# Two attention layers in one kernel: K chunks in halves, wider weighted-V products, a 28-column normalization, and four more score banks on VectorE

## The chip, the cores and the metric

The kernel runs on one core of a Trainium2 chip. The core has five engines that run at their own pace and wait for each other through semaphores: TensorE (PE: matmuls, with a separate row PEld for loading weights), ScalarE (ACT: exponentials), VectorE (DVE: elementwise work, copies and reductions), GpSimd (POOL) and SyncE (SP, which here only issues DMAs). Matmul results go to PSUM, eight banks of 512 fp32 columns by 128 partitions. The metric is the device time of one execution in microseconds, the median of several runs.

## The reference, cut to what matters

Two independent attention layers on 2048 positions of width 448, with 16 heads of 28; their outputs stand side by side.

```
# A: full attention, 16 query heads, one shared K and V
q = (x @ wq) per head;  k = x @ wk;  v = x @ wv          # k, v: 2048 x 28
p = softmax(q @ k.T * 28**-0.5)                          # 16 x 2048 x 2048
outA = (p @ v, heads side by side) @ wo
# B: local attention, window of 8 positions, 2 apart
q, k, v = x @ wqkv per head
logits[s, w] = q[s] . k[s - 2*w] * 28**-0.5   (masked before the start)
outB = (sum_w softmax(logits)[s, w] * v[s - 2*w], heads side by side) @ wo
```

A's softmax has 16 x 2048 x 2048 = 67 million exponentials, and they make up most of the work.

## The kernel before, in words

**A's main loop.** Scores are computed transposed: 128 keys on the partitions, 512 queries on the columns, one PSUM bank. One such bank is a *unit*; there are 1024, ordered by query chunk `sc` (4), group of four heads `t` (4), key block `tb` (16) and head in the group `j` (4). A pair (sc, t) of 64 units is called a head group here; there are 16, numbered 4·sc + t. Units go through a ring of two *slots* (`SLOTS`, line 26): slot 0 is banks 0, 1, 2, slot 1 is banks 3, 4. TensorE fills a slot (`qk`, L847, or L844 in a form that uses the whole array), ScalarE takes the exponential of the slot in one instruction (L864) into one of seven `expT` buffers, and TensorE multiplies the result by V (L910), accumulating in bank 5 (`PVBANK`). A slot can be filled again only once it is read. 1024 units in steps of 3 and 2 make 410 exponentials.

**Banks taken by VectorE.** In some rounds (one round is both slots) the third bank of slot 0 is left out of ScalarE's exponential, which is then 1024 columns wide instead of 1536. VectorE copies that bank out (`d_x`, L943), and for every two such banks runs a polynomial of three instructions over 1024 columns (L953, L955, L957) that gives the same exponentials as bf16 bits. `OFF_AT` (line 41) lists the rounds in each head group: six for the groups in `SIX`, four for the others, 84 banks in all.

**End of a head group** (`a_quad_end`). VectorE transposes bank 5 out (L971), takes the reciprocal of the denominators (L976, column 28 of 32), multiplies (L977), transposes back (L980), and after each fourth group TensorE applies `wo` (L994).

**The head of the kernel** (`a_head`). K is computed in four chunks of 512 positions, the first in two halves of 256 (`KF`). A half has its matmuls (L675), its squares (L682 on ScalarE for chunk 0; a copy L685 and a product L687 on VectorE for the later chunks), a matmul that adds the squares' sum (L689) and an add that writes `kT` (L692). The squares give a factor per key, which `a_v` applies to V: four one-column matmuls (L750) into **the bank of the chunk's last K part**, then an exponential on ScalarE (L754, `gcol`), then `v_aug` (L756 to L762). The bank is free only after L754. In chunk 0 the two query halves and the two K halves take banks out of `HB`, that is 0 to 3.

**B's pipeline.** Sixteen blocks of 128 positions: q and k (L1035, L1040), v (L1050, L1054) through DRAM into a shifted copy `Vsh`; products of q and shifted k (L1076), summed by four-column matmuls (L1085); softmax (L1097 to L1117); products of V and weights for two of the eight window slots at a time (L1130, four per block), summed and transposed on TensorE (L1136), then `wo` (L1143) and the store (L1148). Its work fills what A leaves of VectorE and TensorE.

**What sets the order.** Nothing is ordered at run time: `Sched.run` is a list scheduler in the builder, which simulates five queues with durations written by hand and emits each engine's instructions in the order that it finds. An instruction has a priority `pr` (lower goes first) and an earliest time `rel`. Score groups, their exponentials and the `d_x` copies are the *ring*, whose turn is protected from longer work (`limit`). `area` measures how many matmul columns TensorE ran in the last 2.5 us; where it is low, filler is put in (matmuls on `warm` data: L418, L441, L839) or score groups take the whole-array form. So any changed duration or priority reorders all that follows.

```
SLOTS = ((0, 1, 2), (3, 4))
PVBANK = 5
XBANKS = (6, 7)
SIX = (1, 2, 3, 5, 6, 8, 9, 11, 12, 14)
OFF_AT = {q: (0, 2, 3, 5, 7, 8) if q in SIX else (0, 2, 5, 7) for q in range(1, 16)}
PSTT = -35.0
```

Of the kernel before, what the change touches and what calls it, by code (L numbers as in the profile page):

```python
# [30 lines left out]
TAILB = (4, 0)  # L31
WARM = 8
KF = 256
QT = 27.0


EL, EP, EQ = -10.141819427815111, -5.83493489876537, 4.836063470359898
EOFF = 8
A2 = SCALE * 1.4426950408889634
SIX = (1, 2, 3, 5, 6, 8, 9, 11, 12, 14)  # L40
OFF_AT = {q: (0, 2, 3, 5, 7, 8) if q in SIX else (0, 2, 5, 7) for q in range(1, 16)}
OFF_AT[15] = (0, 2, 3, 5)
OFF_AT[0] = (4, 5, 6, 7)
LATE = 2
PSTT = -35.0
DR = 2
DX = 3

# [50 lines left out]
class Sched:  # L99
# [6 lines left out]
    IDLE = 1400.0  # L106
    FULL = {2: 1400.0, 3: 1300.0}
    LOW = 1200.0
    QKT = 0.32
    EPS = -0.04  # L110
    FILL = None
# [37 lines left out]
    def run(self, engines):  # L149
# [15 lines left out]
        locks = {"dve": 0.0, "gp": 0.0}  # L165

        def area(T):
            return sum(d for (t1, d) in recent if t1 > T - self.WIN) / self.WIN

        def ready(o):  # L170
            t = o.rel
# [210 lines left out]
def t_dve_ps(n):  # L382
    return 0.067 + 1.04e-3 * n
# [22 lines left out]
class Gen:  # L406
# [142 lines left out]
    def consts(self):  # L549
# [40 lines left out]
                                               base=-PAD, pattern=[[0, H], [2, WIN]], channel_multiplier=1), W=["mask0"], pr=-8.05)  # L590
        a("dve", 1.0, lambda e: e.memset(g.wo4[:, :, :], 0.0), W=["wo4"], pr=-3)
        a("gp", 0.2, lambda e: e.memset(g.kTB[:, :, 0:PAD], 0.0), W=["kTBpad"], pr=-8.05)

    def loads(self):
        g, a = self, self.s.add
# [52 lines left out]
              R=[("wq", min(t, 1)), "wqz", ("d_x", 0, 0), ("d_x", 0, 1)], W=[("wq4", t)], pr=-6 if t == 0 else 1.2 + t)  # L648

    HB = (0, 1, 2, 3)  # L650
    TB = (4, 5, 6, 7)
    LB = (6, 7)
    VPR = 0.5
# [3 lines left out]
    def a_head(self):  # L657
        g, a = self, self.s.add
        g.kz_ops = {}
        for n, pr, rel in ((WARM, -30, 0.0), (1, -15, 4.6)):  # L660
            def warm(e, n=n):
                for _ in range(n):
                    r = e.matmul(g.bank(3), g.warm[:, 0:128], g.warm[:, :], start=True, stop=True)  # L663
                return r
            u = Use(f"warm{n}", (3,))
            a("pe", 0.43 * n, warm, R=["warm"], use=u, pr=pr, rel=rel)
        for c in range(NCH):
            pr = -9 if c == 0 else c
            HB = g.HB if c == 0 else g.LB
            if c < 2:  # L670
                g.a_tr(c)
            for k, (lo, n) in enumerate(((0, KF), (KF, 512 - KF)) if c == 0 else ((0, 512),)):
                u = Use(f"K{c}.{k}", HB, late=c == 0)
                for kt in range(4):
                    a("pe", t_mm(n), lambda e, u=u, c=c, kt=kt, lo=lo, n=n: e.matmul(  # L675
                        g.bank(u.bank, n), g.wk4[:, kt, :], g.xT_A[:, kt, 512 * c + lo:512 * c + lo + n],
                        start=kt == 0, stop=kt == 3),
                      R=[("xT", c, kt), "wk4"], W=[u], use=u, pr=pr + 0.1 * k, rel=8.0 * min(c, 1), dense=n)
                ksq = g.k_sq[:, c % 2, lo:lo + n]
                kc = g.kT[:, 512 * c + lo:512 * c + lo + n]  # L680
                if c == 0:
                    a("act", t_act(n), lambda e, u=u, ksq=ksq, n=n: e.activation(ksq, g.bank(u.bank, n), ACT.Square),  # L682
                      R=[u, "d_u"], W=[("k_sq", c % 2, k)], use=u, pr=-100)
                else:
                    a("dve", t_dve_ps(n), lambda e, u=u, kc=kc, n=n: e.tensor_copy(out=kc, in_=g.bank(u.bank, n)),  # L685
                      R=[u], W=[("kT", c, k)], use=u, pr=min(pr, -2))
                    a("dve", t_dve_2x(n), lambda e, ksq=ksq, kc=kc: e.tensor_tensor(out=ksq, in0=kc, in1=kc, op=ALU.mult),  # L687
                      R=[("kT", c, k), "d_u"], W=[("k_sq", c % 2, k)], pr=-2)
                a("pe", t_mm(n), lambda e, u=u, ksq=ksq, n=n: e.matmul(  # L689
                    g.bank(u.bank, n), g.hq[:, 2, :], ksq, start=False, stop=True, skip_group_check=True),  # L690
                  R=[("k_sq", c % 2, k), "hq", "d_u"], W=[u], use=u, pr=pr + 0.1 * k, dense=n)
                a("dve", t_dve_ps(n) + 0.08, lambda e, u=u, kc=kc, n=n: e.tensor_scalar(  # L692
                    out=kc, in0=g.bank(u.bank, n), scalar1=g.cols[:, 0:1], scalar2=None, op0=ALU.add),
                  R=["kadd"], W=[("kT", c, k)], use=u, pr=min(pr, -2) - (1 - k if c == 0 else 0))
            kc = g.kT[:, 512 * c:512 * c + 512]
            g.kz_ops[c] = [a("dve", Lock(0.3), lambda e, j=j, c=c, kc=kc: e.tensor_scalar(
                out=g.kz[:, j, 512 * c:512 * c + 512], in0=kc, scalar1=g.cols[:, 8 + j:9 + j], scalar2=None, op0=ALU.mult),
                R=["jmask"] + g.keys_of(c), W=[("kz", c)], pr=4 + c) for j in range(4)]
            if c == 0:
                g.a_q(0, first=True)  # L700
            g.a_v(c, u)

    def key_of(self, tb):

        return ("kT", tb // 4, int(KF <= 128 * tb < 512))

    def keys_of(self, c):
        return sorted({self.key_of(4 * c), self.key_of(4 * c + 3)})
# [1 line left out]
    def a_tr(self, c):  # L710

        g, a = self, self.s.add
        for kts in ((0,), (1,), (2,), (3,)) if c == 0 else ((0, 1), (2, 3)):
            u = Use(f"T{c}{kts[0]}", g.TB[kts[0]:kts[0] + 1] if c == 0 else g.LB)
            for i, kt in enumerate(kts):
                for b in range(4):
                    a("pe", 0.1, lambda e, u=u, i=i, kt=kt, b=b: e.transpose(  # L717
                        g.psb[:, 1024 * u.bank + 512 * i + 128 * b:1024 * u.bank + 512 * i + 128 * b + 128],
                        g.xst[:, 4 * c + b, XB0[kt]:XB0[kt] + 128], g.ident[:, :]),
                      R=[("xst", c), "ident"], use=u, pr=-16 if c == 0 else -2, dense=128)  # L720
            for i, kt in enumerate(kts):
                dst = g.xT_A[:, kt, 512 * c:512 * c + 512]
                src = lambda u=u, i=i: g.psb[:, 1024 * u.bank + 512 * i:1024 * u.bank + 512 * i + 512]
                if c or kt % 2:
                    a("dve", 0.335, lambda e, src=src, dst=dst: e.tensor_copy(out=dst, in_=src()),
                      W=[("xT", c, kt)], use=u, pr=-2 if c else -9)
                else:
                    a("act", t_act(512), lambda e, src=src, dst=dst: e.activation(dst, src(), ACT.Copy),
                      W=[("xT", c, kt)], use=u, pr=-110)

    def a_v(self, c, uk):

# [201 lines left out]
    def d_exp(self, bank, slot, sib):  # L934
# [11 lines left out]
        o.ring = True  # L946
        o.sib = sib
        if h:
            pp = 10.0 + 26.7 * (4 * g.quad[0] + g.quad[1]) + PSTT
            u, v = g.d_u[:, :], g.d_v[:, :]  # L950
            lo = xx.bitcast(mybir.dt.uint16).rearrange("p (c two) -> p c two", two=2)[:, :, 0]
            di = [("d_x", m % DX, 0), ("d_x", m % DX, 1)]
# [9 lines left out]
    def a_quad_end(self, sc, t, hf=None):  # L962
# [11 lines left out]
        g.evacs = [o]  # L974
        pt = g.PV_T[:, t % 2, :].rearrange("p (b e) -> p b e", e=32)
        a("dve", 0.16, lambda e: e.reciprocal(out=g.rden[:, t % 2, bs], in_=pt[:, bs, DH]), R=kk("PV"), W=kk("rden"), pr=p0)  # L976
        a("dve", t_dve_1x(w), lambda e: e.tensor_tensor(  # L977
            out=g.oN[:, bs, :], in0=pt[:, bs, :], in1=g.rden[:, t % 2, bs].unsqueeze(2).to_broadcast([128, b, 32]), op=ALU.mult),
          R=kk("PV") + kk("rden"), W=[("oN", x) for x in keys], pr=p0)
        a("dve", 0.09 + 1.04e-3 * w, lambda e: e.transpose(  # L980
            out=g.oTn[:, t, cs], in_=g.oN[:, :, :].rearrange("p b e -> p (b e)")[:, cs]),
          R=[("oN", x) for x in keys], W=[("oTn", t, x) for x in keys], pr=p0)
# [80 lines left out]
    def b_logits(self, k):  # L1063
# [1 line left out]
        T = g.B0 + g.BSTEP * k  # L1065
        c, b = k // 4, k % 4
        pr = T + 12
        for t in range(4):
            R = [("qTB", c % 2, t), ("kTB", t, c)]
            if k == 0:  # L1070
                R += ["kTBpad"]
            elif b == 0:
                R += [("kTB", t, c - 1)]
            qv = g.qTB[:, c % 2, t, 128 * b:128 * b + 128].unsqueeze(1).to_broadcast([KC, WIN, 128])
            kv = g.ap(g.kTB[:, t, :], 128 * k, [[2, WIN], [1, 128]])
            op = a("dve", t_dve_2x(1024), lambda e, t=t, qv=qv, kv=kv: e.tensor_tensor(  # L1076
                out=g.prodT[0:KC, t, :, :], in0=qv, in1=kv, op=ALU.mult), R=R, W=[("prodT", t)], pr=pr, rel=T)
            if k == 0:
                op.deps.update(o for i in range(2) for o in g.s.rd.get(("xst", i), ()) if o.eng == "pe")
        u = Use(f"L{k}", XBANKS, spare=128)  # L1080
# [41 lines left out]
    def b_out(self, k):  # L1122
# [1 line left out]
        T = g.B0 + g.BSTEP * k  # L1124
        par, b = (k // 2) % 2, k % 2
        pr = T + 30
        for qr in range(4):
            Vv = g.Vsh[:, k % 2, 2 * qr:2 * qr + 2, :].rearrange("p w (d h) -> p w d h", h=H)
            av = g.a_n[:, par, b, 2 * qr:2 * qr + 2, :].unsqueeze(2).to_broadcast([128, 2, DH, H])
            a("dve", t_dve_2x(2 * D), lambda e, qr=qr, Vv=Vv, av=av: e.tensor_tensor(  # L1130
                out=g.prod2[:, 2 * qr:2 * qr + 2, :].rearrange("p w (d h) -> p w d h", h=H), in0=Vv, in1=av, op=ALU.mult),
              R=[("Vsh", k % 2), ("a_n", par, b)], W=[("prod2", qr)], pr=pr, rel=T)
        u = Use(f"BT{k}", XBANKS)
        for t in range(4):
            for w in range(WIN):
                a("pe", 0.056, lambda e, u=u, t=t, w=w: e.matmul(  # L1136
                    g.bank(u.bank, 128, 128 * t, p1=KC), g.prod2[:, w, KC * t:KC * t + KC], g.ident[:, :],
                    start=w == 0, stop=w == WIN - 1), R=[("prod2", w // 2), "ident"], W=[u], use=u, pr=pr, dense=128).extra = 0.045
        a("dve", t_dve_ps(512), lambda e, u=u: e.tensor_copy(out=g.oT[:, k % 2, :], in_=g.bank(u.bank, p1=KC)),
          W=[("oT", k % 2)], use=u, pr=-1)  # L1140
        u = Use(f"BP{k}", XBANKS)
# [53 lines left out]
```

## Time and profile before

| | |
|---|---|
| median of 13 runs | 451.98 us (449.22 to 465.8) |
| the profiled execution | 451.61 us, of which 449.9 span |
| mean granted TensorE clock | 0.992 of full speed |
| ScalarE busy | 435.3 us (97%), of it L864 430.3 in 410 instructions |
| VectorE busy | 419.0 us (93%) in 680 instructions |
| TensorE busy | 410.1 us (91%) |
| GpSimd busy | 14.0 us (3%) |
| DMA | 27.30 MB, mean 61 GB/s |
| first exponential starts | 10.07 us |

In the rows of the profile, `L864` is a line of the kernel, `expT<-ps` what is written and read, and an arrow in brackets names the instruction whose end released a waiting engine. "Busy" of an engine is the time in which at least one of its instructions is under way; successive instructions of one engine overlap by a little, so the cost of one in a full queue is the distance between two starts, not its duration.

### The profile page before, as it was taken

To read this page: it belongs to the slowest core of one execution; us is meant where nothing else is said; L and a number is where in the kernel's file an instruction comes from. 1 tells how busy PE (TensorE), PEld (TensorE's weight loads), DVE (VectorE), ACT (ScalarE), POOL (GpSimd) and SP (SyncE) were. 2 spreads that over 40 slices of the span, in tenths; PEclk is the share of its full clock that TensorE was granted. 3 is DMA by queue.
4 is the path that set the end of the run, shared out by engine and by line. 5 is a ranking of instruction groups with operands and counts; after the bars stand their busy time and mean duration, and the time that the engine had idled before them with its cause. 6 is when DMAs were issued, how large, how long until landed. Compare 5 with 4: busy or idle time off the path is not lost.

```text
span 449.9 us, 8992 instructions
## 1 busy us (share of the span) xinstructions
PE 410.1 (91%) x3755; PEld 159.1 (35%) x3800; DVE 419.0 (93%) x680; ACT 435.3 (97%) x431; POOL 14.0 (3%) x36
## 2 busy tenths in 40 slices
PE   8888999999899999999999989989989989898894
PEld 4222232322353423323443443334324433442441
DVE  7889999899999999999979999998999998999963
ACT  4899999999999999999999989999999999999995
POOL 6112000000000000000000000000000000000000
PEclk9999999899999999999999989999999999999999
DMA  7946202000261312002121330023000330220001
GB/s 170 191 63 171 38 12 92 1 2 10 93 128 34 103 41 84 12 10 83 34 71 52 96 100 12 12 74 102 12 21 22 103 103 22 83 92 12 12 12 42
DMA packets 39988, 27.30 MB, mean 61 GB/s; under 512 B 15518, under 2 KB 39592, under 8 KB 39948
## 3 DMA queue, kind: packets, MB, share of 16 engines
q1 hardware_dynamic: 37452, 24.06, 19.4%
q0 software_dynamic: 816, 1.53, 1.6%
q10 hardware_dynamic: 1680, 1.13, 0.8%
q8 instruction: 30, 0.49, 0.5%
q14 instruction: 10, 0.08, 0.1%
HBM read 18.06 MB, written 5.52 MB: 52 GB/s over the span
## 4 chain that ended last, share of the span: by engine, by line
ACT 94%; PE 4%; DVE 1%; issue 0%
ACT expT L864 94%; PE ps L663 1%; PE ps L844 1%; PE ps L847 1%; ACT e_t L1111 0%; PE ps L781 0%; PE ps L994 0%; PE ps L910 0%; PE ps L717 0%; DVE qT L800 0%; PE ps L796 0%; PE ps L675 0%; ACT outA L1001 0%; DVE PV_T L971 0%; DVE oTn L980 0%
## 5 line engine op out<-in xcount | busy, mean ns | idle before, releaser
L864 ACT ACTIVATE expT<-ps 128x1024 bf16<-128x1024 f32 (+1 forms) x410 | 430.3, 1337 | 4.3 <-PE ps L847 3.0
L847 PE MATMUL ps<-qT,kT 32*128 32x512 bf16 (+1 forms) x1043 | 152.0, 372 | 22.1 <-ACT expT L864 16.9
L910 PE MATMUL ps<-expT,v_aug 128*32 128x512 bf16 (+1 forms) x1000 | 95.2, 377 | 0.3 <-DVE mx L1097 0.3
L847 PEld LDWEIGHTS ps<-qT,kT 32*128 32x128 bf16 x1043 | 37.9, 91 | 115.8 <-ACT expT L864 103.4
L943 DVE TENSOR_SCALAR d_x<-ps 128x512 f32<-128x512 f32 x84 | 57.2, 680 | 7.1 <-PE ps L847 6.1
L953 DVE SCALAR_TENSOR_TENSOR d_u<-d_x 128x1024 f32<-128x1024 uint16 x42 | 50.8, 1210 | 0.4 <-PE ps L689 0.3
L957 DVE SCALAR_TENSOR_TENSOR dexp<-d_u,d_x 128x1024 int16<-128x1024 f32 x42 | 50.9, 1211 | 0.0
L955 DVE SCALAR_TENSOR_TENSOR d_u<-d_u,d_x 128x1024 f32<-128x1024 f32 x42 | 50.8, 1209 | 0.1
L1136 PE MATMUL ps<-ident,prod 128*112 128x128 bf16 x512 | 46.2, 227 | 0.1
L910 PEld LDWEIGHTS ps<-expT,v_aug 128*32 128x32 bf16 x1000 | 24.1, 93 | 53.2 <-issue 50.3
L1076 DVE TENSOR_TENSOR stage<-qTB,kTB 112x1024 bf16<-112x1024 bf16 x64 | 41.9, 675 | 0.3 <-PE ps L1085 0.3
L1136 PEld LDWEIGHTS ps<-ident,prod 128*112 128x112 bf16 x512 | 35.0, 130 | 19.0 <-issue 17.1
L1130 DVE TENSOR_TENSOR prod<-Vsh,a_n 128x896 bf16<-128x896 bf16 x64 | 37.3, 611 | 0.9 <-PE ps L1136 0.8
L1035 PE MATMUL ps<-xT_B,wqkv 128*128 128x512 bf16 x115 | 35.8, 384 | 1.2 <-issue 0.8
L1085 PEld LDWEIGHTS ps<-ones,stage 112*128 112x128 bf16 x512 | 18.6, 96 | 10.0 <-issue 5.9
L1085 PE MATMUL ps<-ones,stage 112*128 112x4 bf16 x512 | 21.8, 167 | 0.1
L994 PE MATMUL ps<-wo,oTn 128*128 128x448 bf16 x64 | 17.4, 356 | 1.8 <-DVE oTn L980 1.7
L781 PE MATMUL ps<-xT_A,wq 128*128 128x512 bf16 (+1 forms) x60 | 18.3, 378 | 0.4 <-issue 0.3
L1143 PE MATMUL ps<-wo_B,oT 112*128 112x448 bf16 x64 | 18.5, 358 | 0.1
L1050 PE MATMUL ps<-wqv,xT_B 128*128 128x448 bf16 x64 | 17.8, 357 | 0.5 <-DVE qT L800 0.5
L971 DVE STREAM_TRANSPOSE PV_T<-ps 128x512 f32<-128x512 f32 (+1 forms) x17 | 11.5, 678 | 5.8 <-PE ps L910 5.7
L1035 PEld LDWEIGHTS ps<-xT_B,wqkv 128*128 128x128 bf16 x128 | 9.9, 97 | 18.1 <-issue 12.7
(107 smaller groups left out, 282.8 us busy)
## 6 DMA issues: line engine op xcount, KB each, us to landing
Vsh<-v_scratch SPq DMA_DIRECT2D x16, 896.0 KB, 4.6
v_scratch<-Vst SPq DMA_DIRECT2D x16, 112.0 KB, 1.7
out_dram<-outB SPq DMA_DIRECT2D x16, 112.0 KB, 1.7
out_dram<-outA SPq DMA_DIRECT2D x15, 112.0 KB, 1.7
stage<-in_A_x_dram ACTq DMA_DIRECT2D x2, 448.0 KB, 4.1
wqkv<-in_B_wqkv_dram SPq DMA_DIRECT2D x1, 672.0 KB, 5.1
wo_B<-in_B_wo_dram POOLq DMA_DIRECT2D x4, 98.0 KB, 2.8
wo<-in_A_wo_dram POOLq DMA_DIRECT2D x4, 98.0 KB, 2.6
```

Source lines behind the costliest of these rows:

```text
L847: r = e.matmul(g.bank(b0 + i, nq, nq * k), g.kT[32 * j:32 * j + 32, 128 * tb:128 * tb + 128], g.qT[32 * j:32 * j + 32, sc % 2, t, q0:q0 + ...
L864: x = a("act", t_exp(w), lambda e, b0=b0, w=w, n=n: e.activation(g.expT[:, n % ERING, 0:w], g.ps[:, 512 * b0:512 * b0 + w], ACT.Exp, scale ...
L910: x = e.matmul(g.bank(PVBANK, nq, q0, p0=32 * j, p1=32 * j + 32), g.v_aug[:, w, tb, :], src[:, nq * k:nq * k + nq], start=first, stop=last ...
L943: o = a("dve", t_dve_ps(512), lambda e: e.tensor_scalar(out=xx[:, 512 * h:512 * h + 512], in0=g.bank(bank), scalar1=-128.0 * A2, scalar2=1 ...
L953: a("dve", t_dve_1x(1024), lambda e: e.scalar_tensor_tensor(out=u, in0=lo, scalar=EP * F, in1=lo, op0=ALU.add, op1=ALU.mult), R=di, W=["d_ ...
L955: a("dve", t_dve_1x(1024), lambda e: e.scalar_tensor_tensor(out=v, in0=u, scalar=EQ * F * F, in1=lo, op0=ALU.add, op1=ALU.mult), R=["d_u"] ...
L957: a("dve", t_dve_1x(1024), lambda e: e.scalar_tensor_tensor(out=out, in0=v, scalar=EL / F ** 3, in1=xx, op0=ALU.mult, op1=ALU.subtract), R ...
L1035: a("pe", t_mm(512), lambda e, u=u, t=t, kt=kt, w=w: e.matmul(g.bank(u.bank), g.wqkv[:, kt, w * D + KC * t:w * D + KC * t + 128], g.xT_B[: ...
L1076: op = a("dve", t_dve_2x(1024), lambda e, t=t, qv=qv, kv=kv: e.tensor_tensor(out=g.prodT[0:KC, t, :, :], in0=qv, in1=kv, op=ALU.mult), R=R ...
L1085: r = e.matmul(g.bank(u.bank, 128).rearrange("p (h w) -> p h w", w=WIN)[:, 4 * t:4 * t + 4, w], g.prodT[0:KC, t, w, :], g.ones4[:, :], sta ...
L1130: a("dve", t_dve_2x(2 * D), lambda e, qr=qr, Vv=Vv, av=av: e.tensor_tensor(out=g.prod2[:, 2 * qr:2 * qr + 2, :].rearrange("p w (d h) -> p ...
L1136: a("pe", 0.056, lambda e, u=u, t=t, w=w: e.matmul(g.bank(u.bank, 128, 128 * t, p1=KC), g.prod2[:, w, KC * t:KC * t + KC], g.ident[:, :], ...
```

## The change

- K's second chunk is also computed in halves (`KSPLIT = 2`), and the score groups wait for the half that they need (`key_of`). The two K halves of chunk 0 get fixed banks, 2 and 5 (`KB`), so the four columns of `gcol` are now in bank 5. The keys of the dependency tracking are named by half.
- B's products of V and weights take four window slots at a time (`WS = 4`): two instructions per block in place of four.
- The normalization multiplies the 28 columns of each head in place of all 32; `oN` is zeroed once on GpSimd.
- Head groups 10 and 13 join `SIX`: 88 banks on VectorE in place of 84.
- The polynomial instructions of the first four VectorE banks get a priority later by `D0 = 30`.
- Between 14 and 50 us of the plan, `area` is taken 150 lower (`EARLY`).
- `TS = 1` and `TACT` are names for what was there before.

```diff
+KSPLIT = 2
+TS = 1
+WS = 4
+TACT = ((0, 2), ())
...
-SIX = (1, 2, 3, 5, 6, 8, 9, 11, 12, 14)
+SIX = (1, 10, 13, 2, 3, 5, 6, 8, 9, 11, 12, 14)
...
+D0 = 30.0
...
+    EARLY = 150.0
...
-            return sum(d for (t1, d) in recent if t1 > T - self.WIN) / self.WIN
+            return sum(d for (t1, d) in recent if t1 > T - self.WIN) / self.WIN - (self.EARLY if 14 < T < 50 else 0.0)
...
+        a("gp", 0.2, lambda e: e.memset(g.oN[:, :, :], 0.0), W=["oNz"], pr=-8.04)
...
+    KB = ((2,), (5,))
...
-            for k, (lo, n) in enumerate(((0, KF), (KF, 512 - KF)) if c == 0 else ((0, 512),)):
-                u = Use(f"K{c}.{k}", HB, late=c == 0)
+            for k, (lo, n) in enumerate(((0, KF), (KF, 512 - KF)) if c < KSPLIT else ((0, 512),)):
+                u = Use(f"K{c}.{k}", g.KB[k] if c == 0 else g.LB, late=c == 0)
+                uk, x0 = (u, c, k), 0
...
-        return ("kT", tb // 4, int(KF <= 128 * tb < 512))
+        return ("kT", tb // 4, int(tb // 4 < KSPLIT and KF <= 128 * (tb % 4)))
...
-            pp = 10.0 + 26.7 * (4 * g.quad[0] + g.quad[1]) + PSTT
+            pp = 10.0 + 26.7 * (4 * g.quad[0] + g.quad[1]) + PSTT + (D0 if g.nd <= 4 else 0.0)
...
-        a("dve", t_dve_1x(w), lambda e: e.tensor_tensor(
-            out=g.oN[:, bs, :], in0=pt[:, bs, :], in1=g.rden[:, t % 2, bs].unsqueeze(2).to_broadcast([128, b, 32]), op=ALU.mult),
-          R=kk("PV") + kk("rden"), W=[("oN", x) for x in keys], pr=p0)
+        a("dve", t_dve_1x(b * DH), lambda e: e.tensor_tensor(
+            out=g.oN[:, bs, 0:DH], in0=pt[:, bs, 0:DH], in1=g.rden[:, t % 2, bs].unsqueeze(2).to_broadcast([128, b, DH]), op=ALU.mult),
+          R=kk("PV") + kk("rden") + ["oNz"], W=[("oN", x) for x in keys], pr=p0)
...
-        for qr in range(4):
-            Vv = g.Vsh[:, k % 2, 2 * qr:2 * qr + 2, :].rearrange("p w (d h) -> p w d h", h=H)
-            av = g.a_n[:, par, b, 2 * qr:2 * qr + 2, :].unsqueeze(2).to_broadcast([128, 2, DH, H])
-            a("dve", t_dve_2x(2 * D), lambda e, qr=qr, Vv=Vv, av=av: e.tensor_tensor(
+        for w in range(0, WIN, WS):
+            Vv = g.Vsh[:, k % 2, w:w + WS, :].rearrange("p w (d h) -> p w d h", h=H)
+            av = g.a_n[:, par, b, w:w + WS, :].unsqueeze(2).to_broadcast([128, WS, DH, H])
+            a("dve", t_dve_2x(WS * D), lambda e, w=w, Vv=Vv, av=av: e.tensor_tensor(
...
```

## The prediction, made before the result was known

> **What bounds the kernel now.** I read the chain that ended last first, then ScalarE's timeline, then VectorE's, then busy time by stage.
>
> ```profile
> ACT 94%; PE 4%; DVE 1%; issue 0%
> ```
>
> ScalarE's exponentials (L864) carry 94% of the span, from 10.07 us to about 443 us. So the end moves in three ways only: fewer columns on ScalarE, less waiting between exponentials, or a changed head or tail. The start of the row, from ScalarE's timeline (start, duration, engine, line; idle time before in brackets):
>
> ```profile
> 10.07 1.45 ACT L864 ACTIVATE expT<-ps 128x1536 bf16<-128x1536 f32 x1 [1.19 <-PE ps L847]
> 11.41 0.17 ACT L754 ACTIVATE gcol<-ps 128x4 f32<-128x4 f32 x1
> 12.33 1.45 ACT L864 ACTIVATE expT<-ps 128x1536 bf16<-128x1536 f32 x1 [0.75 <-PE ps L847]
> 13.68 1.02 ACT L864 ACTIVATE expT<-ps 128x1024 bf16<-128x1024 f32 x1
> 14.58 1.46 ACT L864 ACTIVATE expT<-ps 128x1536 bf16<-128x1536 f32 x1
> 15.91 1.04 ACT L864 ACTIVATE expT<-ps 128x1024 bf16<-128x1024 f32 x1
> 17.44 1.02 ACT L864 ACTIVATE expT<-ps 128x1024 bf16<-128x1024 f32 x1 [0.48 <-PE ps L847]
> ```
>
> Start to start, 1024 columns take 0.90 us (13.68 to 14.58) and 1536 take 1.33 us (14.58 to 15.91): one bank of 512 costs 0.43 us. The widths show that the slots do not alternate here: 1536 follows 1536, then 1024 follows 1024, so each time the same banks are used twice running and ScalarE waits for their refill. The price, against these steps: 12.33 − 11.41 − 0.06 for gcol = 0.86 us, and 17.44 − 15.91 − 0.90 = 0.63 us. Why the order broke stands in TensorE's timeline:
>
> ```profile
> 11.57 0.39 PE L839 MATMUL ps<-warm 128*128 128x512 bf16 x1 [0.22 <-ACT gcol L754]
> 11.89 0.61 PE L847 MATMUL ps<-qT,kT 32*128 32x512 bf16 x5
> ```
>
> L839 is the filler that opens a score group, and writes the first bank of its slot. It waited for gcol, whose four columns lie in the bank of K's second half: slot (3, 4) could not be filled before gcol, and the five matmuls at 11.89 are both slots at once.
>
> Apart from this, I summed ScalarE's start-to-start distances less 0.90, 1.33, 0.06 (gcol) and 0.31 (L1111): what remains is 1.46 us from 80 to 90 us, 1.82 us from 260 to 270 us, and about 0.13 us per 10 us elsewhere. The two lumps are the clock; busy time by stage (PE, PEld, DVE, ACT and POOL busy us with their instructions, then the granted clock, DMA share and GB/s):
>
> ```profile
> 78.00:80.00 2.00, 1.80 (x42) 1.14 (x38) 2.00 (x4) 2.00 (x3) 0.00 (x0) 1.00 0.03 8
> 80.00:82.00 2.00, 1.52 (x12) 0.43 (x13) 2.00 (x6) 1.79 (x3) 0.00 (x0) 0.65 0.00 0
> 82.00:84.00 2.00, 2.00 (x10) 0.39 (x6) 1.64 (x3) 1.89 (x3) 0.00 (x0) 0.50 0.00 0
> ```
>
> So a clock dip costs 1.3 to 1.7 us.
>
> **The change, part by part.** The sum is against the profiled execution: 451.61 us, a span of 449.9 and 1.7 around it. The median of 13 runs is 451.98, 0.37 above.
>
> *K's first chunk to banks 2 and 5.* Its second half and gcol leave bank 3, so slot (3, 4) can be filled right after the first score group, at about 10.0. Bank 5's first user is a transpose whose copy ends before K's matmuls at 7.3; its next, the first weighted-value product, comes at 15.07, after gcol at 11.58. Nothing new is queued. Gain 0.86; bounds 0 (another hold on the slot) and 0.9. I take 0.86, since the trace names the waiter.
>
> *K's second chunk in halves.* With alternation restored, the second wait goes as well, if the keys are there. The seventh exponential is the first that needs the second chunk (keys from 512 on). It would start at about 16.8 instead of 18.36, and its score matmuls must start by 16.2. Today the keys are ready at 16.80, after a cast of 0.60, a square of 0.33, a matmul of 0.39 and an add of 0.66: too late by 0.6. Halved, the first half's ops shorten by 0.27, 0.13, 0.12 and 0.27 (the 256-wide add takes 0.39 start to start), together 0.8: ready at about 16.0. VectorE pays three more instructions of 0.07 to 0.13, about 0.3 us, in a stretch with idle time (14 to 16 us is 1.37 busy of 2.00). Gain 0 to 0.63; I take 0.5, as the margin is only 0.2. Without the halves, the first gain would largely be paid back here.
>
> *D0.* The first two polynomial pairs (L953 to L957) get lower priority. At 27.65 such an op of 1.13 stood ahead of the last chunk's add (28.79), whose keys now are wanted some 1.5 us earlier, near 29.0, instead of at 30.5; they came at 29.54. It is cover for the same gain: 0 by itself, up to 0.5 lost without it.
>
> *Four more banks to VectorE* (two heads' groups, 10 and 13, from four to six). ScalarE: four exponentials of 1536 become 1024, 4 × 0.43 = 1.72 us. All of it is on the path. VectorE's price, from its timeline:
>
> ```profile
> 407.45 0.61 DVE L1130 TENSOR_TENSOR prod<-Vsh,a_n 128x896 bf16<-128x896 bf16 x1
> 407.98 0.68 DVE L943 TENSOR_SCALAR d_x<-ps 128x512 f32<-128x512 f32 x1
> 408.58 1.21 DVE L957 SCALAR_TENSOR_TENSOR dexp<-d_u,d_x 128x1024 int16<-128x1024 f32 x1
> 409.72 0.61 DVE L1130 TENSOR_TENSOR prod<-Vsh,a_n 128x896 bf16<-128x896 bf16 x1
> ```
>
> An eviction holds the engine 0.60, a polynomial op 1.13. Four evictions and two pairs of three ops: 2.4 + 6.8 = 9.2 us. Some more weighted-value groups of about 0.4 us go to TensorE, idle 40 us in all.
>
> *Four-slot products.* 64 become 32. [...] A transposing matmul (L1136) now waits for a product of 1.0 instead of 0.53, and score matmuls behind it in TensorE's order with it; such waits are 0.7 us in all today, off the chain: 0, at worst 0.7 more.
>
> *28 columns.*
>
> ```profile
> L977 DVE TENSOR_TENSOR oN<-PV_T,rden 128x512 bf16<-128x512 f32 x15 | 10.3, 684 | 0.2
> L977 DVE TENSOR_TENSOR oN<-PV_T,rden 128x256 bf16<-128x256 f32 x2 | 0.8, 424 | 0.1
> ```
>
> 260 ns for 256 columns, so 64 fewer save 0.065: 15 × 0.065 + 2 × 0.03 = 1.0 us of VectorE, of which 0.03 is in the tail. The zeroing on GpSimd (0.2 to 0.5 by its rows) falls in its idle 3.26 us before 11.65.
>
> *VectorE's account*: +9.2 − 2.2 − 1.0 + 0.3 = +6.3 us, against 30.9 idle. By stage (VectorE busy, instructions, clock, DMA):
>
> ```profile
> 92.00:119.00 27.00, 27.00 (x39) 1.00 0.03 10
> 282.00:309.00 27.00, 26.64 (x44) 1.00 0.14 44
> 361.00:389.00 28.00, 26.79 (x45) 1.00 0.16 51
> 416.00:443.00 27.00, 19.09 (x28) 1.00 0.06 19
> ```
>
> The two stages that take the work have 0.4 and 1.2 us to spare for 4.6 each, so B's work slides back into the last stage, which has 7.9. B's last store is issued at 437.05 and A's last at 447.44; slid by 3 to 6 us, B's still comes first. Full stages seem to cost nothing: from 92 to 119 VectorE has no idle time and ScalarE's remainder is 0.13; groups with six banks average 0.30 (dips apart), those with four 0.30.
>
> *EARLY* lowers the measured activity by 150 between 14 and 50 us of the plan, so TensorE gets more filler there. [...]
>
> Sum: −0.86 − 0.5 − 1.72 − 0.03 + 0.2 = −2.9: 448.7 on the profiled run, 449.1 on the median. I forecast 448.9.
>
> **The rivals.** *(1) The start keeps its waits.* The halves come late or another chunk's keys do: 1.36 is not gained, 448.9 + 1.36 = 450.3. For it: margins of 0.2 us, and VectorE full from 16 us on. Against it: the named waiter. *(2) Slower: VectorE becomes the bound in groups 10 and 13.* Evictions (L943) arrive late, slot (0, 1, 2) is not refilled during the 0.90 us of the other slot, and ScalarE waits. If nothing can slide, the overflow is (4.6 − 0.4) + (4.6 − 1.2) = 7.6 us: 448.9 + 7.6 = 456.5; it decides once more than half of that cannot slide (2.9 cancels the gain, 5.2 makes it clearly slower). For it: 99% busy there. Against it: 92 to 119 us, and B's products there are not due soon. *(3) The dips shift.* The whole order of instructions is new; one dip fewer gives 447.4, none 445.9, one more 450.4.
>
> **How the numbers follow.** About 0.5% (2.3 us; 449.7 and 454.2) is what a measurement of this kernel can tell from no change. Forecast 0.58 (own range 447.4 to 450.2, by the bounds of the K halves and EARLY), rival 1 0.19, rival 2 0.11, fewer dips 0.12. Faster: most of the forecast (0.48), fewer dips 0.12, a little of rival 1 (0.05): 0.65. Same: 0.10 + 0.14 = 0.24. Slower: 0.11. The range leaves out rival 2 and the extreme of fewer dips: 446.6 to 452.0.
>
> **What would show it.** Right: widths alternate 1536, 1024 from the first exponential, with no gap over 0.2 us before 20 us; 117 exponentials of 1536 and 88 evictions; L1130 32 times at about 1.08 us; VectorE near 425 us busy. Wrong: a wait on L692 near the seventh exponential or near 29 us (rival 1); L847 waiting for L943, with gaps at 280 to 390 us (rival 2); more or fewer stages with a clock of 0.5 (rival 3).

## The result, and the profile after

446.77 us (median of 11 runs, 446.65 to 447.14) against 451.97 us (median of 48 runs): a ratio of 0.9893, with a 95% interval of 0.9866 to 0.9919. The profiled execution of the changed kernel took 446.72 us, with a span of 444.9. The forecast was 448.9 with a range of 446.6 to 452.0: the right sign, but 5.2 us gained where 3.1 were forecast.

The row with the shares of the chain that ended last still belongs to ScalarE:

```profile
ACT 93%; PE 3%; DVE 3%; DMA 0%; issue 0%
```

Its first rows, from ScalarE's timeline taken in narrow windows (a row with x2 is the named exponential and the one behind it):

```profile
10.13 1.45 ACT L872 ACTIVATE expT<-ps 128x1536 bf16<-128x1536 f32 x1 [1.18 <-PE ps L855]
11.47 0.17 ACT L762 ACTIVATE gcol<-ps 128x4 f32<-128x4 f32 x1
11.53 1.03 ACT L872 ACTIVATE expT<-ps 128x1024 bf16<-128x1024 f32 x1
12.43 2.39 ACT L872 ACTIVATE expT<-ps 128x1536 bf16<-128x1536 f32 x2
13.76 2.40 ACT L872 ACTIVATE expT<-ps 128x1024 bf16<-128x1024 f32 x2
14.66 2.42 ACT L872 ACTIVATE expT<-ps 128x1536 bf16<-128x1536 f32 x2
15.99 2.43 ACT L872 ACTIVATE expT<-ps 128x1024 bf16<-128x1024 f32 x2
```

The widths now alternate, with starts 0.90 and 1.33 us apart and no wait. TensorE fills both slots at once as soon as the first keys are there, nearly two microseconds before gcol:

```profile
9.69 0.60 PE L855 MATMUL ps<-qT,kT 32*128 32x512 bf16 x5 [0.18 <-DVE kT L700]
```

The same three stages as before (PE, PEld, DVE, ACT and POOL busy, then clock, DMA share, GB/s): the clock is whole, with TensorE *less* busy than before in the stage ahead of the first dip, 1.39 us for 1.80. (In the two stages behind it the kernel before ran at a lower clock, 0.65 and 0.50: there a lone matmul of 512 columns, L796, took 0.61 us, and 0.39 at the full clock.)

```profile
78.00:80.00 2.00, 1.39 (x14) 0.34 (x10) 2.00 (x3) 2.00 (x3) 0.00 (x0) 1.00 0.00 0
80.00:82.00 2.00, 1.50 (x12) 0.50 (x12) 1.87 (x5) 2.00 (x4) 0.00 (x0) 1.00 0.00 0
82.00:84.00 2.00, 1.87 (x12) 0.48 (x11) 2.00 (x3) 2.00 (x3) 0.00 (x0) 1.00 0.00 0
```

VectorE's groups, the product and the normalization (count, busy us, mean ns, idle time before):

```profile
L1139 DVE TENSOR_TENSOR prod<-Vsh,a_n 128x1792 bf16<-128x1792 bf16 x32 | 34.1, 1077 | 0.4 <-PE ps L1145 0.4
L985 DVE TENSOR_TENSOR oN<-PV_T,rden 128x448 bf16<-128x448 f32 x15 | 9.2, 611 | 0.2
```

The product takes 1.08 us, as forecast. From start to start in a full queue it is 1.002 us, where a two-slot one took 0.535: 896 more elements take 0.467, which leaves 0.068 in each product beside its elements. VectorE's busy time in the stages shown before, the later ones shifted by the 5 us that they now come earlier:

```profile
92.00:119.00 27.00, 26.82 (x39) 1.00 0.12 38
277.00:304.00 27.00, 26.71 (x41) 1.00 0.14 44
356.00:384.00 28.00, 27.83 (x42) 1.00 0.16 50
411.00:438.00 27.00, 20.61 (x31) 1.00 0.05 15
```

VectorE is now 97.5 to 99.6% busy from 30 us to 410 us, taken in four stretches. It is busy 423.9 us in all, 4.9 more than before.

**Where the time went**, profile against profile, with the start-to-start account of the prediction (waits are what is left of ScalarE's distances after the steps of 0.90, unrounded 0.903, 1.33, 0.06 and 0.31):

| part | before | after | difference, us |
|---|---|---|---|
| first exponential | 10.07 | 10.13 | +0.06 |
| waits before 20 us | 1.53 | 0.00 | −1.53 |
| four exponentials from 1536 to 1024 columns | 121 wide | 117 wide | −1.71 |
| waits near the two clock dips | 1.37 + 1.79 | none | −3.16 |
| all other waits | 4.59 | 5.59 | +1.00 |
| from the last exponential's start to the end | 6.83 | 7.24 | +0.41 |
| span | 449.85 | 444.93 | −4.9 |

The row of the dips says too much. Of the first 1.37 us, a wait of 0.27 ended at 80.36 us, before the clock fell at 80.59; and the profiled run with its two dips took 451.61 us against 449.22 for the fastest, so the two together cost 2.4 us. Some 0.8 of the +1.00 in the row below it is therefore only a matter of where a wait is booked.

The runs say the same without the trace. The kernel before has a lowest group of runs, 449.22 to 449.29, with a mean clock of 0.996 to 0.999, and others above it in steps, down to a clock of 0.947. The changed kernel has only runs with a clock of 0.996 to 1.000. Lowest against lowest the gain is 449.22 − 446.65 = 2.6 us; the rest of the 5.2 is dips that no longer come. Below, "lowest" is the fastest run of a kernel; in each kernel but after_sparse its listed clock is at least 0.996. The kernel before, measured beside every experiment, had a lowest of 449.22 everywhere but beside no_d0, same_order_single, all_groups and ts2, which ran on another chip, where it was 449.56; so about 0.3 us of the distances given for these four is not theirs.

### The profile page after: what moved, and what is told of

Same layout as the page of the kernel before. It is cut to its first block, busy times and chain, and to the rows that moved or that the text cites. A ratio compares the mean times of both kernels' runs of the same rounds, so it can differ in the third digit from the quotient of the medians.

```text
span 444.9 us, 8974 instructions
## 1 busy us (share of the span) xinstructions
PE 409.1 (92%) x3755; PEld 158.7 (36%) x3794; DVE 423.9 (95%) x661; ACT 433.0 (97%) x431; POOL 14.7 (3%) x37
## 3 DMA queue, kind: packets, MB, share of 16 engines
q0 software_dynamic: 816, 1.53, 1.6%
## 4 chain that ended last, share of the span: by engine, by line
ACT 93%; PE 3%; DVE 3%; DMA 0%; issue 0%
ACT expT L872 92%; PE ps L671 1%; DVE kz L704 1%; ACT e_t L1120 1%; PE ps L855 1%; DVE kT L700 0%; DVE d_x L951 0%; DMA out_dram<-outA 0%; DVE qT L808 0%; PE ps L683 0%; PE ps L725 0%; PE ps L918 0%; DVE kT L693 0%; PE ps L789 0%; DVE d_u L695 0%
## 5 line engine op out<-in xcount | busy, mean ns | idle before, releaser
L872 ACT ACTIVATE expT<-ps 128x1024 bf16<-128x1024 f32 (+1 forms) x410 | 428.2, 1354 | 1.3 <-PE ps L855 1.2
L855 PE MATMUL ps<-qT,kT 32*128 32x512 bf16 (+1 forms) x1047 | 153.2, 372 | 21.1 <-ACT expT L872 17.1
L918 PE MATMUL ps<-expT,v_aug 128*32 128x512 bf16 (+1 forms) x996 | 95.5, 376 | 0.2
L855 PEld LDWEIGHTS ps<-qT,kT 32*128 32x128 bf16 x1047 | 38.4, 91 | 118.2 <-ACT expT L872 102.4
L951 DVE TENSOR_SCALAR d_x<-ps 128x512 f32<-128x512 f32 x88 | 59.8, 679 | 0.8 <-PE ps L855 0.3
L965 DVE SCALAR_TENSOR_TENSOR dexp<-d_u,d_x 128x1024 int16<-128x1024 f32 x44 | 53.4, 1213 | 0.1
L963 DVE SCALAR_TENSOR_TENSOR d_u<-d_u,d_x 128x1024 f32<-128x1024 f32 x44 | 53.3, 1212 | 0.1
L961 DVE SCALAR_TENSOR_TENSOR d_u<-d_x 128x1024 f32<-128x1024 uint16 x44 | 53.3, 1212 | 0.0
L1145 PE MATMUL ps<-ident,prod 128*112 128x128 bf16 x512 | 48.2, 227 | 0.7 <-DVE lg L1108 0.6
L918 PEld LDWEIGHTS ps<-expT,v_aug 128*32 128x32 bf16 x996 | 24.6, 93 | 53.1 <-issue 50.5
L1043 PE MATMUL ps<-xT_B,wqkv 128*128 128x512 bf16 x118 | 37.2, 384 | 0.7 <-issue 0.6
L1139 DVE TENSOR_TENSOR prod<-Vsh,a_n 128x1792 bf16<-128x1792 bf16 x32 | 34.1, 1077 | 0.4 <-PE ps L1145 0.4
L1094 PEld LDWEIGHTS ps<-ones,stage 112*128 112x128 bf16 x512 | 16.7, 96 | 7.5 <-issue 5.4
L1094 PE MATMUL ps<-ones,stage 112*128 112x4 bf16 x512 | 19.3, 167 | 0.0
L979 DVE STREAM_TRANSPOSE PV_T<-ps 128x512 f32<-128x512 f32 (+1 forms) x17 | 11.5, 677 | 4.0 <-PE ps L918 4.0
```

Source lines behind the costliest of these rows:

```text
L855: r = e.matmul(g.bank(b0 + i, nq, nq * k), g.kT[32 * j:32 * j + 32, 128 * tb:128 * tb + 128], g.qT[32 * j:32 * j + 32, sc % 2, t, q0:q0 + ...
L872: x = a("act", t_exp(w), lambda e, b0=b0, w=w, n=n: e.activation(g.expT[:, n % ERING, 0:w], g.ps[:, 512 * b0:512 * b0 + w], ACT.Exp, scale ...
L918: x = e.matmul(g.bank(PVBANK, nq, q0, p0=32 * j, p1=32 * j + 32), g.v_aug[:, w, tb, :], src[:, nq * k:nq * k + nq], start=first, stop=last ...
L951: o = a("dve", t_dve_ps(512), lambda e: e.tensor_scalar(out=xx[:, 512 * h:512 * h + 512], in0=g.bank(bank), scalar1=-128.0 * A2, scalar2=1 ...
L961: a("dve", t_dve_1x(1024), lambda e: e.scalar_tensor_tensor(out=u, in0=lo, scalar=EP * F, in1=lo, op0=ALU.add, op1=ALU.mult), R=di, W=["d_ ...
L963: a("dve", t_dve_1x(1024), lambda e: e.scalar_tensor_tensor(out=v, in0=u, scalar=EQ * F * F, in1=lo, op0=ALU.add, op1=ALU.mult), R=["d_u"] ...
```

## The experiments

The twelve runs ask which of the table's rows belongs to which edit. My theory was the prediction's: three gains on ScalarE's chain (start, columns, dips) with VectorE's extra work hidden; the rivals were that VectorE is the bound, and that another edit or the new order itself made the difference. Undoing an edit makes the builder plan the whole order anew, so each such run shows the edit *and* a new plan. Two runs keep the changed kernel's order fixed and change only what is issued in it.

### The start

**no_k**: after, with `KSPLIT = 1` and chunk 0's halves in `HB`.

```diff
-KSPLIT = 2
+KSPLIT = 1
-                u = Use(f"K{c}.{k}", g.KB[k] if c == 0 else g.LB, late=c == 0)
+                u = Use(f"K{c}.{k}", g.HB if c == 0 else g.LB, late=c == 0)
```

> The changed kernel with its K part undone: the second chunk whole and the first chunk's halves back in banks 0 to 3. My theory: the two waits at the start (0.86 and 0.63 us) come back and the rest of the sum stays, so about 446.8 + 1.0 to 1.5 = 447.8 to 448.3 us, with 1536 after 1536 in ScalarE's first rows. Rival (the gain at the start is paid back later, by the 0.23 and 0.28 us that the changed profile shows at 23 and 31 us): at most +1.0. Rival (the dips of the clock went because of the K part): runs between 448 and 452, with a clock of 0.992.

Measured: 453.74 us (lowest 452.44). The two waits are back to the hundredth: 0.86 and 0.62, 1.54 us before 20 us. But the loss is 5.8 us lowest against lowest. The profile splits it: first exponential 0.3 later, the start 1.5, other waits 1.2 (one of 1.15 at 128 us), the end after the last exponential 2.5 (9.8 us instead of 7.2). The profiled run also has two dips, with waits of 1.34 and 1.69 us, and five of the seven runs have a clock below 0.996. The start is as stated; the rest came with the new plan.

**before_kb**: before, with only the banks changed.

```diff
-            HB = g.HB if c == 0 else g.LB
...
-                u = Use(f"K{c}.{k}", HB, late=c == 0)
+                u = Use(f"K{c}.{k}", ((2,), (5,))[k] if c == 0 else g.LB, late=c == 0)
```

> The kernel before with one edit: the two K halves of chunk 0 in banks 2 and 5. My theory: the exponentials alternate from the first on, and of the first wait of 0.86 and the second of 0.63 us the first goes and part of the second stays, because the second chunk's keys are whole (ready near 16.8, wanted at 16.2): last exponential 0.9 to 1.4 us earlier, dip-free time about 448.0 us against 449.2. Rival: the wait moves in full to the second chunk's keys, and the dip-free time is 449 us or more.

Measured: 450.74 us, lowest 450.39, which is 1.2 us more than the kernel before's lowest. The rival was right: the first wait is gone and a single one of 1.33 us stands in front of the first exponential that needs the second chunk. The add on VectorE:

```profile
17.13 0.75 DVE L691 TENSOR_SCALAR kT<-ps,cols 128x512 bf16<-128x512 f32 x1 [0.45 <-PE ps L688]
```

and TensorE's score matmuls behind it:

```profile
17.94 0.60 PE L846 MATMUL ps<-qT,kT 32*128 32x512 bf16 x5
```

The whole chunk's keys are written at 17.13 to 17.88, and the score matmuls start at 17.94. In the changed kernel the first half's keys are written at 15.06 to 15.54, and the seventh exponential starts at 16.89 without a wait. So banks and halves are worth something only together: 1.53 with both, 0.18 with the banks alone.

**no_d0**: after, with `D0 = 0`.

> The changed kernel without the later priority of the first two polynomial pairs. My theory of the prediction: 0 to 0.5 us at the keys of the last chunk (a wait before the exponential near 30 us), so 446.7 to 447.2 us if the rest of the plan comes out alike. Rival (what a re-planned order does at the end and to the clock outweighs the edit, as in the other re-planned versions): 448 us or more, with the loss after 50 us.

Measured: 453.90 us, lowest 453.25. Its profiled execution fell into long dips later on, so only its first 50 us are read. VectorE:

```profile
29.02 1.22 DVE L961 SCALAR_TENSOR_TENSOR d_u<-d_x 128x1024 f32<-128x1024 uint16 x1
30.15 0.75 DVE L700 TENSOR_SCALAR kT<-ps,cols 128x512 bf16<-128x512 f32 x1
```

ScalarE:

```profile
31.71 1.02 ACT L872 ACTIVATE expT<-ps 128x1024 bf16<-128x1024 f32 x1 [1.30 <-PE ps L855]
```

A polynomial op of 1.1 us stands ahead of the last chunk's add, and the exponential behind those keys waits 1.48 us in all; in the changed kernel the wait at this place is 0.28. D0 covers 1.2 us, where the prediction allowed 0.5. The other 5.4 us came with the new plan.

### VectorE's account

**ten_groups**: after, with `SIX` as before (84 banks).

> The changed kernel with 84 banks on VectorE (head groups 10 and 13 with four). My theory: four exponentials are 0.43 us longer, 446.8 + 1.7 = 448.5 us, nothing else. Rival (VectorE is close to being the bound, and its fuller queue costs waits on the score groups): less than +1.2, since those waits go with the four banks. Rival (dips come back with this order): spread over 2 us with a clock below 0.996.

Measured: 449.10 us, lowest 448.75: 2.1 to 2.3 us more. This plan has the changed kernel's waits up to 200 us to within 0.02 us at the large ones (0.22 at 23 us, 0.39 at 194), so this is the cleanest of the undone edits. The last exponential starts 2.0 us later: 1.71 for the columns and 0.36 for waits, less 0.07 at the first exponential. So moving four more banks costs ScalarE nothing in these two plans.

**narrow_dve**: after, with `WS = 2` and 32 columns, planned anew.

> The changed kernel with two-slot products and 32-column normalization: VectorE has 2.2 + 1.0 = 3.2 us more to do, ScalarE nothing. My theory: these savings only pay for the four banks and lie beside ScalarE, so 446.8 to 447.3 us, and VectorE's busy time rises from 423.9 to about 427. Rival (VectorE is the second bound): +1 to +3 us, with L855 waiting for L951 more than the 3.2 us of the changed profile.

Measured: 449.68 us, lowest 449.58, 2.9 us more. By the number alone the rival wins, but the rows of the end (one timeline of all engines; VectorE's last, then SyncE's DMA issue) show how:

```profile
446.39 0.62 DVE L1155 CAST outB<-ps 128x448 bf16<-128x448 f32 x1 [1.02 <-PE ps L1152]
447.05 0.33 SPq L1157 DMA_DIRECT2D out_dram<-outB  x1
```

B's last store is issued 2.3 us behind A's (444.75), so B ends the kernel; 9.1 us pass after the last exponential. L855's weight loads wait only 2.1 us for L951, less than the 3.2 of the changed kernel. Whether the extra 3.2 us of VectorE work or the plan put B there, this run can't say; the next can.

**same_order_narrow**: the changed kernel's order on every engine, but each four-slot product issued as two, and 32 columns.

```diff
-            a("dve", t_dve_2x(WS * D), lambda e, w=w, Vv=Vv, av=av: e.tensor_tensor(
-                out=g.prod2[:, w:w + WS, :] ...
+            a("dve", t_dve_2x(WS * D), lambda e, w=w, Vv=Vv, av=av: [e.tensor_tensor(
+                out=g.prod2[:, w + i:w + i + 2, :] ... for i in (0, 2)][-1],
```

> The changed kernel's order on every engine kept as it is, but each four-slot product issued as two of two slots, and 32 columns multiplied: VectorE pays the 3.2 us that the two edits save, with no new planning. Theory 1 (VectorE is the second bound: its order is full, and the re-planned version without the savings lost 2.9 us for this reason): last exponential and end 1.5 to 3 us later, 448.2 to 449.7 us, and L855 waits longer for L951. Theory 2 (the savings lie beside ScalarE and the 2.9 us came from the new plan alone, whose last B block fell behind A's end): 446.7 to 447.3 us.

Measured: 446.83 us, lowest 446.70, 0.06 more than the changed kernel, while VectorE is busy 426.1 us instead of 423.9. Theory 2. The two savings are worth nothing by themselves in this order, and narrow_dve's 2.9 us came with its plan.

**same_order_single**: the same, with each product issued as four.

> As the run before with the changed kernel's order kept: now each four-slot product is issued as four of one slot, and 32 columns are multiplied, so VectorE pays 96 more fixed parts of 0.07 plus 1.0, about 7.7 us, for the same result. The kept order with 3.2 us more ended 0.06 us later. If VectorE's slack (the changed profile has 21 us idle, of it some 10 before 410 us) still takes it, under 447.5 us; if it decides from somewhere between 3 and 8 us, 448 to 452 us, with ScalarE's waits on late evictions, that is L855 waiting for L951 far above 5 us.

Measured: 449.83 us, lowest 449.66, 3.0 us more, with VectorE busy 430.0 us (6.1 more). So the slack ends between 2.2 and 6.1 us of extra busy time. The added time is not at the end (7.05 us after the last exponential) but in ScalarE's waits: twenty-one of over 0.15 us where the changed kernel has eight, four of them (1.9 us) at a dip in this profiled run; the lowest runs, at a clock of 0.998 to 0.999, are without one. TensorE's waits for L951 (weight loads and matmuls together) go from 3.5 us in the changed kernel over 5.9 in same_order_narrow to 7.0: late evictions take part, but less than was expected. What grows more is the wait of the weighted values (L918) for the last polynomial (L965). Of the weight loads alone (total us, number, longest), first in the changed kernel, then here:

```profile
PEld ps L918 <- DVE dexp L965: 1.8, 5, 0.6
PEld ps L918 <- DVE dexp L965: 5.9, 15, 0.7
```

In same_order_narrow it is 2.2. Score matmuls behind these in TensorE's order wait with them.

**all_groups**: after, with groups 4 and 7 in `SIX` too (92 banks), planned anew.

> The changed kernel with head groups 4 and 7 at six banks as well: 92 banks on VectorE. ScalarE has 1.72 us less to do, VectorE 9.2 us more. If VectorE still has room: 445.0 us, better than both kernels. If its room is used up (the changed kernel has 11 us idle from 30 to 437 us): B's work slides behind A's end, the tail after the last exponential grows from 7 to over 9 us, and the end is at 447 to 450 us.

Measured: 453.12 us, lowest 452.86, 6.2 us more. 10.2 us pass after the last exponential, as expected; but also one wait of 3.42 us, at the end of head group 7. VectorE:

```profile
229.71 1.22 DVE L965 SCALAR_TENSOR_TENSOR dexp<-d_u,d_x 128x1024 int16<-128x1024 f32 x1
231.97 0.70 DVE L979 STREAM_TRANSPOSE PV_T<-ps 128x512 f32<-128x512 f32 x1
```

ScalarE:

```profile
233.42 1.02 ACT L872 ACTIVATE expT<-ps 128x1024 bf16<-128x1024 f32 x1 [3.30 <-PE ps L918]
```

Read it backwards: ScalarE waits for L918, the weighted values of the *next* group, which free an `expT` buffer. They wait until bank 5 has been transposed out (231.97). That comes after the weighted values of the group's last polynomial (229.71), and after an eviction and a copy for B which stood ahead of it on VectorE (230.84 and 231.44). Meanwhile ScalarE fills its seven buffers and stops. So a late polynomial and a full queue at a group's end, and not only a late eviction, are a way in which VectorE becomes the bound.

**ts2**: after, with `TS = 2`.

> The changed kernel with B's products of q and k two head quarters at a time (32 instructions of 2048 elements for 64 of 1024): VectorE saves 32 x 0.07 = 2.2 us, ScalarE nothing. By the account that such savings lie beside ScalarE: no gain by itself, 446.3 to 447 us where the new plan comes out as well, 448 to 450 us where it lets B's last block fall behind A's end or lets dips back in.

Measured: 451.47 us, lowest 450.46, 3.8 us more, although VectorE has less to do (421.4 us busy). The tail is 6.7 us; but one wait of 3.78 us stands at 368.3, by the same mechanism (L872 waiting 3.42 for L918; L979 at 367.10, the last polynomial at 364.84).

No version tried beats the changed kernel.

### The clock

**no_early**: after, with `EARLY = 0`.

> The changed kernel without the lowered activity between 14 and 50 us. My theory: this edit is worth little by itself, 446.3 to 447.3 us, and the dips stay away because the whole order is new. Rival (EARLY keeps the clock up): one to two dips of 1.3 to 1.7 us in most runs, 448 to 450 us with a spread of some us.

Measured: 450.21 us; 8 of 16 runs lie within 0.03 us of 449.65, the others between 450.75 and 464.45; six have a clock below 0.996, down to 0.952. Both statements fail in part: dips are back in six runs, but not in the other ten, and the lowest time is 3.0 us above the changed kernel's too. Its profiled run, one with a long dip, has 9.8 us after the last exponential: 2.6 of the 3.0.

**before_dense** and **after_sparse**: 150 taken off the measured activity throughout, in the kernel before; 150 added throughout, in place of EARLY, in the changed one.

```diff
 before_dense
-            return sum(d for (t1, d) in recent if t1 > T - self.WIN) / self.WIN
+            return sum(d for (t1, d) in recent if t1 > T - self.WIN) / self.WIN - 150.0
 after_sparse
-  - (self.EARLY if 14 < T < 50 else 0.0)
+  - (-150.0)
```

> The kernel before with its measured TensorE activity taken 150 lower throughout, so more filler everywhere; nothing else. [...] Theory 2 (filler has nothing to do with the dips, or its cost eats the gain): dips in two thirds of the runs as before, or an undisturbed time above 451 us.

> The changed kernel with the activity taken 150 higher throughout (the opposite of EARLY), so less filler. Theory 1 (filler keeps the clock up): dips in most runs, median 448.5 to 452 us, clock 0.985 to 0.993. Theory 2 (the dips have another cause): clock 0.997 or more as in the changed kernel, 446.2 to 447.5 us.

Measured: before_dense 450.81 us, lowest 450.67, 22 runs with no clock below 0.996, where of the 35 runs of the kernel before beside it 25 were below. after_sparse 457.58 us, six runs with clocks of 0.928 to 0.987. The granted clock on the page of before_dense (tenths of full speed, 40 slices):

```profile
PEclk9999999999999999999999999999999999999999
```

and on the page of after_sparse:

```profile
PEclk9999999999689999999999999999999997998899
```

In before_dense what the edit made is plain: 61 filler matmuls for 49, and 87 score matmuls in the whole-array form for 45. (They are counted by their weight loads after the warm-up. Some of the traces lack records of dense matmuls: the kernel before's has 39 fillers for 49 weight loads, the changed kernel's has 28, same_order_narrow's has 38 for the same order on TensorE, and the weight loads are 38 in both.) So here the clock stays up, at 0.996 or more in all 22 runs, in the version with more columns on TensorE. after_sparse points the same way, with 18 whole-array scores for 41 and 35 filler matmuls for 38. In both the rest of the order is new too: after_sparse also has a wait of 2.9 us at 371 us. The cover is not free: before_dense has more of small waits than the kernel before, and 7.7 us after the last exponential in place of 6.8. Lowest against lowest it is 1.45 us slower, and its median is level with the 451.07 of the kernel before beside it: what it saves in dips it pays for elsewhere.

## Why the prediction was right, and where it was off

- *Banks and halves*, −0.86 − 0.5: measured −1.53 before 20 us. The named waiter was right, and so was the statement that without the halves the gain would be paid back (before_kb). The halves gave all of 0.63, as the keys came at 15.54, not 16.0. Against it stand 0.23 us at 23 us and 0.28 at 31 us, where the next chunks' keys are wanted earlier, and 0.06 at the first exponential: about −1.0 net.
- *D0* was sized at up to 0.5 of cover; it covers 1.2.
- *Four banks*, −1.72: measured −1.71 by the widths, and 2.0 by the last exponential of ten_groups.
- *VectorE's account*, hidden: right for the size of this change. Its busy time rose by 4.9, not 6.3. That it has a limit was right too, and rival 2's price (it cancels the gain once VectorE has 2.9 us too much) fits what was seen: 2.2 us more of busy time cost nothing, 6.1 more cost 3.0. Its way was right only in part: the waits that grow most are those for the last polynomial, and the largest (3.4 and 3.8 us) come from the seven `expT` buffers behind a late group end.
- *The four-slot saving*, 2.2 in VectorE's account: the author's estimate. The two profiles together give the same: by the distances between starts given above, 64 × 0.535 − 32 × 1.002 = 2.2 us. (The group's busy time fell by more, 37.3 − 34.1 = 3.2, because it counts the overlapping ends as well.)
- *The tail*, −0.03: measured +0.41. ScalarE's last copy starts 4.45 us after the last exponential, before it was 3.84. Two things make up the difference:

```profile
439.85 0.58 DVE L1012 CAST outA<-ps 128x448 bf16<-128x448 f32 x1
442.14 0.54 ACT L1009 ACTIVATE outA<-ps 128x448 bf16<-128x448 f32 x1 [3.58 <-DMA out_dram<-outA]
```

  The last normalization stood behind a copy of `outA` on VectorE, which put the last matmuls 0.33 us back, and then ScalarE's copy waited nearly 0.3 us more for a store that still read its buffer. The last store landed 0.2 us sooner after its issue than before. The prediction's account of the tail has no term for the store that holds `outA`.
- *EARLY and the dips*, +0.2: this is the term that was mis-sized. The +0.2 and its bounds were the author's estimate, and no run shows them: no_early is 3.0 us slower than the changed kernel, lowest against lowest, but with another plan. The two dips, which cost 2.4 us by the runs, are gone in all twelve runs of the changed kernel. The text had this as rival 3 with a chance of 0.12, and its "none" at 445.9. The undisturbed gain, 2.6 us, is 0.3 from the sum of 2.9; the rest of the 5.2 is dips. With the dips left as they were the median would have been about 451.97 − 2.6 = 449.4 us (an estimate from these runs). That the measured 446.77 lies 2.1 us below the forecast, at the very end of the range, is the plan's luck with the clock and not the argument's merit.

What removed the dips is not settled, and it is not shown to be EARLY. Filler and whole-array scores by their weight loads after the warm-up, and the runs with a mean clock below 0.996:

| kernel | filler | whole-array scores | runs below 0.996 |
|---|---|---|---|
| before | 49 | 45 | 25 of 35 |
| before_dense | 61 | 87 | 0 of 22 |
| changed | 38 | 41 | 0 of 12 |
| same_order_single | 38 | 41 | 4 of 12 |
| no_early | 40 | 41 | 6 of 16 |
| ts2 | 43 | 55 | 6 of 12 |
| after_sparse | 35 | 18 | 6 of 6 |

The changed kernel has less of both than the one before, and no dips. same_order_single has the changed kernel's order on TensorE, with a later VectorE beside it, and dips again. Every version of the changed kernel that was planned anew has some runs below 0.996, whichever edit was undone or added. And between 14 and 50 us, where EARLY acts, the changed kernel has two filler matmuls and two whole-array scores where no_early has none, while the dip in no_early's profile comes at 337 us. So neither EARLY nor the amount of filler decides alone; which stretches of which order let the clock fall stays open. Open too is how the planner came by its ends: in no_k, no_early, narrow_dve and all_groups 9.1 to 10.2 us pass after the last exponential, in the changed kernel 7.2.

The undone edits do not add up: the losses of no_k, no_early, narrow_dve, ten_groups and no_d0, lowest against lowest, are 5.8, 3.0, 2.9, 2.1 and 6.6 us for a change whose undisturbed gain is 2.6. Each was measured with a plan that had not been chosen for it.

## What to carry to other kernels

Where a builder plans the order of everything, an ablation measures the edit plus another plan: keep the order and change what is issued in it, or read the edit's own place in the trace, before believing the difference. A wait that is taken away at the head of a pipeline shows its worth only once the next input is early enough as well; look for the next deadline before counting it. And look at the spread of the runs before: here they reach from 449.22 to 466.86 us, with clocks down to 0.947, and 2.75 us of the median of 451.97 lie above the fastest run. The changed order lost that part (no run with a clock below 0.996) and another brought it back (no_early, 6 of 16) without anyone having planned it.

## What the runs showed of the hardware that was not expected

In the profiled runs the clock stayed at half for 3.413 us in a dip of the kernel before and of no_k (two dips each) and of narrow_dve, 6.83 in the one of same_order_single, 10.24, 6.83 and 6.83 in the three of after_sparse, 17.07 in the one of no_early, and 10.24 and 20.48 in the two of no_d0: one, two, three, five and six times 3.413. The mean granted clock of longer stretches goes with it: 0.98 from 30 to 130 us in the kernel before, where 3.413 us at half lie in 100, and 0.89 from 330 to 410 us in no_early, where 17.07 lie in 80. The two dips of the kernel before begin 184.32 us apart, 54 times 3.413, and those of no_k 139.95, 41 times. (Left out is the half clock at the very end, from 442.95 us on in the changed kernel, which outlasts the span.) In the longest dip of after_sparse TensorE's row is full, and the clock stays at half all the same, with the columns as before:

```profile
117.00:120.00 3.00, 3.00 (x18) 0.63 (x15) 2.27 (x4) 2.86 (x3) 0.00 (x0) 0.59 0.12 16
120.00:123.00 3.00, 3.00 (x20) 1.46 (x17) 2.83 (x6) 2.05 (x2) 0.00 (x0) 0.50 0.85 290
123.00:126.00 3.00, 3.00 (x25) 1.97 (x23) 0.56 (x1) 2.48 (x2) 0.00 (x0) 0.50 0.00 0
```

This dip went from 117.54 to 127.78 us, with TensorE busy 3.00 of 3.00 in each row shown. So in this run a row full of busy time did not show that the clock would come back.
